# A gated attention kernel: x in contiguous chunks, three rows a head in one transfer, and a new order at the end

## The chip, the cores and the metric

The kernel runs on one core of one Trainium2 chip. The metric is device time in microseconds (us), the median of several executions. One execution was also recorded by the hardware profiler, and every line of a profile below comes from such a recorded execution. The engines are TensorE (PE, with its weight loads PEld), VectorE (DVE), ScalarE (ACT), GpSimd (POOL) and SyncE (SP), which here only issues transfers.

## The reference

With S = 2048 tokens, D = 512 features and 32 heads of 16:

```python
g = sigmoid((x * gate_w).sum(-1, keepdims=True))
qkv = x @ wqkv                                   # 512 -> 3 * 512
p = softmax(q @ k.T * 16 ** -0.5)                # per head, 2048 x 2048
a = concat_heads(p @ v) @ wo
r = x @ w_r
idx = argsort(-r)[:2]                            # two tokens of all
y = (silu(x[idx] @ w_gate) * (x[idx] @ w_up)) @ w_down * sigmoid(r[idx])
b = x; b[idx] += y
out = g * a + (1 - g) * b
```

Everything is float32, in and out.

## The kernel before, in words

Projections, the output product and the low-order corrections are made of pairs of float32r tiles: a value is split into a high part (`hi`, a copy by ACT into float32r) and a low part (`lo`, the value minus `hi`, by VectorE or GpSimd). A product is then three matmuls: hi x hi, hi x lo, lo x hi. `split` (L68) is that helper; `pool_split` (L76) does both parts on GpSimd.

The order of instructions is written out by hand; nothing is reordered later, so each engine's queue runs in the order in which the Python code issues.

**Start.** 14 matmuls on a zero tile `warm` (L228) keep TensorE busy while the first loads run. `load_w(0)` (L112) loads the weights of k, then x's first block (`load_x(0)`, L135), then the weights of q. x is kept transposed, features on partitions, in four blocks of 512 tokens (`nb`), each of four chunks of 128 features (`c`); a chunk is 256 KB, and in DRAM its 128 rows of 2 KB lay 8 KB apart. All of these are issued by SP. `split_x` (L140) makes the high and low parts of a block, the low part of chunk 3 on GpSimd, the others on VectorE. `proj0` (L221) is one projection of 128 columns for one block: twelve matmuls, first the eight that need only x's high parts (two a chunk), then the four with its low parts; it goes into one of three rotating PSUM banks (`st`). In this order come k0, q0, k1, k2, k3, q1, q2 (the digit is the block). After each, ACT writes the high part and VectorE the low part of the result (`ev`, `evx`), which is the only reader of the PSUM bank. `first_rows` (L209) copies the rows of the first two heads from there straight into the attention tiles `Kx[0]` and `Qx[0]`, some of them from GpSimd's queue; `store_ev` (L190) stores everything to DRAM scratch (`qk_scr`), from which later heads are loaded. The weights of V (`wvs`) are split after k1's projection, the low parts in turn on VectorE and GpSimd; the high parts lie in `Kx[1]`.

**Attention tiles.** A head takes 48 partitions in `Kx` (k high, k low, k high) and in `Qx` (q high, q high, q low), so that one matmul over 48 rows gives all three products; two more rows carry the negated row maxima. Two heads form a pair (partitions 0 and 64), and a pair is done in two units of 1024 queries. In DRAM scratch the high and the low parts were two separate planes, so that `load_k` (L257) and `load_q` (L266) needed two transfers a head: one of 32 rows, one of 16.

**Lead phase** (steps -21 to -1, 27 to 90 us). TensorE takes in turn score matmuls for the first maxima (`m_lead`, L609), the last projection of the first group (q3) and the products for V (`v_part`, L291, three a step). Beside it GpSimd multiplies the x rows (`xn`, from `load_rows`, L313) with the router and gate weights (`products`, L322), and ACT sums them (`sums`); TensorE reads the sums in `r_row` (L339, matmul L341) at the last step.

**Main loop** (512 steps of 128 keys). A hand-written pattern (`ORDER`) mixes score matmuls (L669, exponentials on ACT at L670), score matmuls for the maxima 21 steps ahead (L589, reduced on VectorE at L593), the products with V (L679) and filler work: the projections of the other three groups, the routed tokens' layers, the output product. Maxima go through `m_rows` (L652), eight small transfers on SP for each unit. `evict` (L201) stores a projected group part; `split_at` (L498) prepares a group of attention outputs for the output product, on GpSimd.

**End.** `tail` (L780) handles the last unit: the last three products of tiles 10, 11 and 9 for what is already there (`late_wo`), the normalisation of the last heads' outputs, their split, and their product with `wz` (L820) for tiles 12 to 15, three matmuls a tile. `finish` (L557) is one VectorE operation that adds a tile from PSUM; `acc_add` (L471) does the same by ACT and GpSimd. `store` (L561) writes a 256 KB tile of the output.

## Time and profile before

| | |
|---|---|
| median of 3 runs | 1420.77 us (1420.66 to 1420.93) |
| profiled execution | 1419.9 us, span of the trace 1417.9 us |
| mean granted TensorE clock | 0.999 |
| PE busy | 1410.2 us (99%) |
| DVE busy | 1288.8 us (91%) |
| ACT busy | 1170.9 us (83%) |
| POOL busy | 320.4 us (23%) |
| moved by DMA | 92.87 MB, 65 GB/s over the span |

The profiled execution's time lies 2.0 us above its span: the span runs from the first to the last event that the trace holds. Lines of the timeline and of the chain begin with the start and the length in us; `x4` is a merged run of four instructions; what stands in brackets is the engine's idle time before it and what ended that. Rows of a wait list give the total, the number and the longest. Rows of the table by stage give the length of the stage, then busy time (and instructions) of PE, PEld, DVE, ACT and POOL, the granted clock, the mean busy share of the 16 DMA engines, and GB/s.

### The profile page before, as it was taken

Reading aid. Unit: us, or ns where it says so; the run is one execution under the profiler, and the core shown is the slowest. Engines: PE = TensorE matmul, PEld = TensorE weight load, DVE = VectorE, ACT = ScalarE, POOL = GpSimd, SP = SyncE. Lnnn points to the kernel's source line nnn. Section 1 sums busy time; section 2 is a strip of 40 time slices with the busy share of each in tenths; the row PEclk is TensorE's granted clock in tenths of the full one; section 3 lists DMA queues with packets and bytes.
Section 4 is the critical chain, followed back from the end, with each engine's and each line's share of the span. In section 5 each row is a group of like instructions: output and inputs, shape, how many; then the busy total and the mean of one; then the engine's idle time right before and its main releaser. Section 6 shows DMA issues by size and latency. Waiting matters only on the chain.

```text
span 1417.9 us, 24172 instructions
## 1 busy us (share of the span) xinstructions
PE 1410.2 (99%) x9113; PEld 630.7 (44%) x9113; DVE 1288.8 (91%) x1532; ACT 1170.9 (83%) x2276; POOL 320.4 (23%) x337
## 2 busy tenths in 40 slices
PE   9999999999999999999999999999999999999998
PEld 6654444444444444444444444434444444444433
DVE  6889999999999999999999999999999999999943
ACT  5568888888888888888888888888888888888986
POOL 4851101102000001200000100043722322234411
PEclk9999999999999999999999999999999999999999
DMA  8601121212223221312222332424322131012012
GB/s 242 235 27 51 30 42 31 66 34 51 46 64 97 62 54 31 68 30 65 58 83 54 87 82 78 105 58 120 83 46 54 34 69 28 26 31 58 10 35 93
DMA packets 51592, 92.87 MB, mean 65 GB/s; under 512 B 14208, under 2 KB 21376, under 8 KB 49844
## 3 DMA queue, kind: packets, MB, share of 16 engines
q1 hardware_dynamic: 51188, 91.02, 24.4%
q8 instruction: 72, 1.18, 0.4%
q0 software_dynamic: 288, 0.30, 0.1%
q14 instruction: 44, 0.36, 0.1%
HBM read 63.77 MB, written 28.57 MB: 65 GB/s over the span
## 4 chain that ended last, share of the span: by engine, by line
PE 98%; DVE 0%; DMA 0%; ACT 0%; SPq 0%; issue 0%; POOL 0%; DVEq 0%; ACTq 0%
PE av L679 36%; PE st L669 24%; PE mxa L589 12%; PE mxb L589 10%; PE fl L154 6%; PE fl L508 4%; PE st L298 3%; PE st L154 2%; PE mxa L624 1%; PE fl L399 1%; DMA xs<-xT 0%; PE fl L437 0%; DVE acc L559 0%; DVE Mr L593 0%; PE mxa L508 0%; PE mxb L624 0%
## 5 line engine op out<-in xcount | busy, mean ns | idle before, releaser
L670 ACT ACTIVATE P<-st 128x512 f32<-128x512 f32 x2028 | 1065.6, 599 | 191.4 <-PE st L669 108.0
L593 DVE TENSOR_REDUCE Mr<-mxa 128x2 f32<-128x1024 f32 x655 | 795.7, 1215 | 2.6 <-PE mxa L589 2.5
L679 PE MATMUL av<-P,V 128*32 128x512 f32 x4096 | 545.6, 605 | 0.0
L669 PE MATMUL st<-Qx,Kx 50*128 50x512 f32 x2028 | 536.5, 444 | 0.8 <-ACT P L670 0.6
L593 DVE TENSOR_REDUCE Mr<-mxb 128x1 f32<-128x512 f32 x654 | 450.9, 689 | 61.0 <-PE st L669 17.1
L669 PEld LDWEIGHTS st<-Qx,Kx 50*128 50x128 f32 x2028 | 279.0, 184 | 239.6 <-ACT P L670 223.8
L589 PE MATMUL mxb<-Kx,Qx 48*128 48x512 f32 x654 | 325.1, 497 | 0.0
L589 PE MATMUL mxa<-Kx,Qx 48*128 48x512 f32 x1310 | 294.7, 417 | 0.0
L589 PEld LDWEIGHTS mxb<-Kx,Qx 48*128 48x128 f32 x654 | 119.5, 183 | 273.7 <-DVE Mr L593 273.7
L589 PEld LDWEIGHTS mxa<-Kx,Qx 48*128 48x128 f32 x1310 | 124.8, 183 | 43.6 <-DVE Mr L593 2.6
L679 PEld LDWEIGHTS av<-P,V 128*32 128x32 f32 x4096 | 81.2, 108 | 139.3 <-issue 133.2
L205 POOL TENSOR_SCALAR ev<-pe 128x512 fp32r<-128x512 f32 x24 | 35.7, 1490 | 411.6 <-ACT pe L203 411.6
L475 POOL TENSOR_TENSOR acc<-acc,w 128x512 f32<-128x512 f32 x36 | 46.1, 1280 | 202.1 <-ACT w L474 202.0
L77 POOL TENSOR_SCALAR hl<-m 128x16 fp32r<-128x16 f32 x31 | 7.8, 252 | 294.1 <-DVE m L640 294.1
L154 PE MATMUL fl<-xh,wh 128*128 128x512 f32 x96 | 42.9, 447 | 0.0
L154 PE MATMUL fl<-xh,wl 128*128 128x512 f32 x96 | 40.4, 421 | 0.0
L508 PE MATMUL fl<-woh,ahl 128*128 128x512 f32 x96 | 35.2, 447 | 0.0
L559 DVE SCALAR_TENSOR_TENSOR acc<-fl,gg,acc 128x512 f32<-128x512 f32 x11 | 8.2, 747 | 27.9 <-PE fl L508 27.9
L629 DVE TENSOR_REDUCE Mr<-mxa 128x2 f32<-128x1024 f32 x21 | 25.7, 1222 | 8.4 <-PE mxa L624 8.4
L154 PE MATMUL fl<-xl,wh 128*128 128x512 f32 x96 | 32.6, 421 | 0.0
L300 ACT ACTIVATE V<-st 128x512 f32<-128x512 f32 x16 | 9.6, 600 | 27.8 <-PE st L298 27.8
L206 POOL TENSOR_TENSOR ev<-pe,ev 128x512 fp32r<-128x512 f32 x24 | 30.8, 1284 | 2.0
(192 smaller groups left out, 780.0 us busy)
## 6 DMA issues: line engine op xcount, KB each, us to landing
q_scr<-ev SPq DMA_DIRECT2D x15, 512.0 KB
Kx<-k_scr SPq DMA_DIRECT2D x30, 256.0 KB
Qx<-q_scr SPq DMA_DIRECT2D x54, 128.0 KB
k_scr<-ev SPq DMA_DIRECT2D x13, 512.0 KB
Qx<-q_scr SPq DMA_DIRECT2D x70, 64.0 KB
xs<-xT SPq DMA_DIRECT2D x16, 256.0 KB
xn<-x SPq DMA_DIRECT2D x4, 1024.0 KB
Qx<-hr SPq DMA_DIRECT2D x256, 2.0 KB
```

The lines of the kernel that those rows point to most:

```text
L154: nc.tensor.matmul(ps, a[:, i, c, :], b[nb][:, c, :], start=n == 0, stop=n == 11)
L205: nc.gpsimd.tensor_scalar(ev[:, 0], t, 1.0, None, op0=OP.mult)
L206: nc.gpsimd.tensor_sub(ev[:, 1], t, ev[:, 0].bitcast(F32))
L298: nc.tensor.matmul(ps, a[nb][:, c, sl], b[:, c, :], start=c == 0 and n == 0, stop=c == 3 and n == 2)
L475: nc.gpsimd.tensor_add(a, a, w)
L508: nc.tensor.matmul(ps, a[:, sl], b[:a.shape[0], c, :], start=first and n == 0, stop=last and n == 2)
L589: nc.tensor.matmul(dst, Qx[u % 3][64 * j:64 * j + 48, t * 128:t * 128 + 128], k_of(u, t // 4)[64 * j:64 * j + 48, c * 512:c * 512 + 512], ...
L593: nc.vector.tensor_reduce(Mr[:, g0:g0 + (2 if r == 1 else 1)], MX[r - 1], axis=AX.X, op=OP.max, negate=True)
L629: nc.vector.tensor_reduce(*r, axis=AX.X, op=OP.max, negate=True)
L669: nc.tensor.matmul(ps, k, q, start=True, stop=True)
L670: nc.scalar.activation(P[s][:, 2 * j + c, :], ps, AF.Exp)
L679: nc.tensor.matmul(AV[0][32 * ct:32 * ct + 32, :], V[:, kt, h * VW:h * VW + 32], P[s][:, ct, :], start=kt == 0, stop=kt == KT - 1)
```

## The change

1. x lies in DRAM so that each chunk of 128 features by 512 tokens is one contiguous 256 KB; of the first block, chunks 0 and 2 are issued by ACT, the others by SP as before.
2. All low parts of x are made by VectorE. V's weights are split later, two chunks after k2's projection and two after k3's, the low parts all on GpSimd.
3. Ten warming matmuls instead of fourteen.
4. The scratch of q and k holds a head's rows as they stand in the attention tiles, three for each feature (k: high, low, high; q: high, high, low). `store_ev` therefore writes three rows where it wrote two, in two transfers; `load_k` and `load_q` fetch a head with one transfer of 48 rows. The first pair's q keeps the order that `first_rows` gives its k, with two transfers.
5. At the end: tile 11 is added by `finish` and not by `acc_add`; the matmuls of tiles 12 and 13 with the high parts come first; the last tile is added and stored in two halves, one from ACT's queue, one from SP's.
6. The first `split_at` is issued three steps later.

```diff
-    qk_scr = {n: dram.tile([2, D, S], F32R, name=f"{n}_scr") for n in "qk"}
+    qk_scr = {n: dram.tile([D, 3, S], F32R, name=f"{n}_scr") for n in "qk"}
...
-            nc.sync.dma_start(xst[nb][:, c], ap(xT, c * 128 * S + nb * 512, [[S, 128], [1, 512]]))
+            eng = nc.scalar if nb == 0 and c % 2 == 0 else nc.sync
+            eng.dma_start(xst[nb][:, c], ap(xT, (nb * 4 + c) * 128 * 512, [[512, 128], [1, 512]]))
...
-            split(xh[nb][:, c], xl[nb][:, c], xst[nb][:, c], lo_engine=nc.gpsimd if c == 3 else None)
+            split(xh[nb][:, c], xl[nb][:, c], xst[nb][:, c])
...
-        nc.sync.dma_start(
-            ap(qk_scr[which], g * 128 * S + nb * 512, [[S, 128], [D * S, 2], [1, 512]]).bitcast(F32), ev.bitcast(F32))
+        e = ev.bitcast(F32)
+        for i, src in ((0, e), (2, e[:, 0, :])) if which == "k" else ((0, e[:, 0:1, :].to_broadcast([128, 2, 512])), (2, e[:, 1, :])):
+            d = ap(qk_scr[which], (g * 384 + i) * S + nb * 512, [[3 * S, 128], [S, 2 - i // 2], [1, 512]])
+            nc.sync.dma_start(d.bitcast(F32), src)
...
-    for _ in range(14):
+    for _ in range(10):
...
-    for c in range(4):
-        split(wv[1][:, c], wv[2][:, c], wvs[:, c], lo_engine=nc.gpsimd if c % 2 else None)
...
-            o = (g * 128 + r + 16 * j) * S
+            o = (g * 128 + r + 16 * j) * 3 * S
-            nc.sync.dma_start(t[64 * j:64 * j + 32, :], ap(qk_scr["k"], o, [[S, 16], [D * S, 2], [1, S]]).bitcast(F32))
-            nc.sync.dma_start(t[64 * j + 32:64 * j + 48, :], ap(qk_scr["k"], o, [[S, 16], [1, S]]).bitcast(F32))
+            nc.sync.dma_start(t[64 * j:64 * j + 48, :], ap(qk_scr["k"], o, [[S, 48], [1, S]]).bitcast(F32))
...
-                nc.sync.dma_start(t[64 * j:64 * j + 32], ap(qk_scr["q"], o, [[S, 16], [0, 2], [1, n]]).bitcast(F32))
-                nc.sync.dma_start(t[64 * j + 32:64 * j + 48], ap(qk_scr["q"], D * S + o, [[S, 16], [1, n]]).bitcast(F32))
+                if pair:
+                    nc.sync.dma_start(t[64 * j:64 * j + 48], ap(qk_scr["q"], o, [[S, 48], [1, n]]).bitcast(F32))
+                else:
+                    nc.sync.dma_start(t[64 * j:64 * j + 32], ap(qk_scr["q"], o, [[3 * S, 16], [S, 2], [1, n]]).bitcast(F32))
+                    nc.sync.dma_start(t[64 * j + 32:64 * j + 48], ap(qk_scr["q"], o + 2 * S, [[3 * S, 16], [1, n]]).bitcast(F32))
...
-        acc_add(11, pw[1], gg)
+        finish(11, pw[1])
...
-        for t in range(4):
-            for n, (a, b) in enumerate(((0, 0), (1, 0), (0, 1))):
-                nc.tensor.matmul(banks[t], hl[a][:, t * 128:t * 128 + 128], wz[0][:, b, :], start=n == 0, stop=n == 2)
-            finish(12 + t, banks[t])
-            store(12 + t)
+        for t, n in ((0, 0), (0, 1), (1, 0), (1, 1), (0, 2), (1, 2), (2, 0), (2, 1), (2, 2), (3, 0), (3, 1), (3, 2)):
+            a, b = ((0, 0), (0, 1), (1, 0))[n]
+            nc.tensor.matmul(banks[t], hl[a][:, t * 128:t * 128 + 128], wz[0][:, b, :], start=n == 0, stop=n == 2)
+            if n == 2 and t < 3:
+                finish(12 + t, banks[t])
+                store(12 + t)
+        a = acc[3][:, 3, :]
+        for i, eng in enumerate((nc.scalar, nc.sync)):
+            c = slice(256 * i, 256 * i + 256)
+            nc.vector.scalar_tensor_tensor(a[:, c], banks[3][:, c], gg[:, 15:16], a[:, c], op0=OP.mult, op1=OP.add)
+            eng.dma_start(out[15 * 128:, c], a[:, c])
...
-        at_step(now[0] + 10, split_at, 0, (0, 1))
+        at_step(now[0] + 13, split_at, 0, (0, 1))
...
     for w, nb in (("k", 2), ("k", 3), ("q", 1), ("q", 2)):
         proj0(w, nb)
+        if w == "k":
+            for c in (2 * nb - 4, 2 * nb - 3):
+                split(wv[1][:, c], wv[2][:, c], wvs[:, c], lo_engine=nc.gpsimd)
...
-        "xT": np.ascontiguousarray(x.T), "x": x, "wqkv": wqkv,
+        "xT": np.ascontiguousarray(x.T.reshape(4, 128, 4, 512).transpose(2, 0, 1, 3)), "x": x, "wqkv": wqkv,
```

More of the change, by code (lines that the diff above doesn't have):

```diff
@@ L271, in load_q @@
             for j in range(2):
-                o = (pair * 32 + 16 * j) * S + q0
+                o = (pair * 32 + 16 * j) * 3 * S + q0
                 t = Qx[u % 3][:, i * n:i * n + n].bitcast(F32)
-                nc.sync.dma_start(t[64 * j:64 * j + 32], ap(qk_scr["q"], o, [[S, 16], [0, 2], [1, n]]).bitcast(F32))
-                nc.sync.dma_start(t[64 * j + 32:64 * j + 48], ap(qk_scr["q"], D * S + o, [[S, 16], [1, n]]).bitcast(F32))
+                if pair:
[3 more added lines that the diff above has]
+                    nc.sync.dma_start(t[64 * j + 32:64 * j + 48], ap(qk_scr["q"], o + 2 * S, [[3 * S, 16], [1, n]]).bitcast(F32))
     def k_of(u, c):
```

## The prediction

> **What bounds the kernel now.** I read the page first, then the waits of TensorE, the table by stage, and the chain that ended last in order of time.
>
> ```profile
> span 1417.9 us, 24172 instructions
> PE 1410.2 (99%) x9113; PEld 630.7 (44%) x9113; DVE 1288.8 (91%) x1532; ACT 1170.9 (83%) x2276; POOL 320.4 (23%) x337
> PE 98%; DVE 0%; DMA 0%; ACT 0%; SPq 0%; issue 0%; POOL 0%; DVEq 0%; ACTq 0%
> ```
> ```profile
> PE st L229 <- DVE warm L226: 1.2, 1, 1.2
> PE st L669 <- ACT P L670: 0.6, 2, 0.4
> PE st L154 <- ACT xh L70: 0.6, 1, 0.6
> PE st L820 <- DVE onl L71: 0.3, 1, 0.3
> ```
> ```profile
> 200.00:600.00 400.00, 400.00 (x2647) 174.65 (x2639) 380.35 (x443) 337.49 (x651) 50.88 (x54) 1.00 0.22 53
> ```
> ```profile
> 2.59 5.46 DMA xs<-xT
> 8.07 0.64 ACT xh L70
> 8.75 18.58 PE st L154 x78
> 27.33 0.43 PE mxa L624 x2
> ```
>
> TensorE is on the chain for 98% of it and idle for 1417.9 - 1410.2 = 7.7 us in all; from 200 to 600 us it has no gap. The whole list of its waits is 2.7 us long, and two of the four lie where the change works: the first projection waits for x, the last product waits for VectorE. The chain starts with the first x block's last chunk landing at 8.05 and is TensorE from 8.75 on. So a gain can come from the first 27 us and the last 10 us alone, and the middle can only be harmed.
>
> **The start, up to 27 us.** Four stalls are to be priced.
>
> ```profile
> 1.18 5.33 PE L229 MATMUL st<-warm 128*128 128x512 bf16 x14 [1.18 <-DVE warm L226]
> 3.46 0.63 ACT L70 ACTIVATE wh<-ws 128x512 fp32r<-128x512 f32 x1 [1.45 <-DMA ws<-wqkv]
> 4.57 1.95 PE L229 MATMUL st<-warm 128*128 128x512 bf16 x6
> 8.78 1.29 POOL L71 TENSOR_TENSOR xl<-xs,xh 128x512 fp32r<-128x512 f32 x1 [3.14 <-ACT xh L70]
> 9.50 1.12 DVE L71 TENSOR_TENSOR wl<-ws,wh 128x512 fp32r<-128x512 f32 x1 [1.40 <-ACT wh L70]
> 10.10 2.68 ACT L70 ACTIVATE xh<-xs 128x512 fp32r<-128x512 f32 x4 [0.63 <-DMA xs<-xT]
> 10.46 0.40 PE L154 MATMUL st<-xh,wh 128*128 128x512 f32 x1
> 10.76 2.06 DVE L71 TENSOR_TENSOR xl<-xs,xh 128x512 fp32r<-128x512 f32 x3
> 13.30 0.39 PE L154 MATMUL st<-xh,wh 128*128 128x512 f32 x1
> 16.02 0.39 PE L154 MATMUL st<-xh,wh 128*128 128x512 f32 x1
> 18.74 0.68 DVE L74 SCALAR_TENSOR_TENSOR evx<-st,evx 128x512 fp32r<-128x512 f32 x1
> 20.52 2.19 ACT L70 ACTIVATE Kx<-wvs 128x512 fp32r<-128x512 f32 x4 [1.95 <-DMA wvs<-wqkv]
> 21.46 0.39 PE L154 MATMUL st<-xh,wh 128*128 128x512 f32 x1
> 24.30 0.50 PE L154 MATMUL st<-xh,wh 128*128 128x512 f32 x1
> ```
>
> The rows at 10.46, 13.30, 16.02, 21.46 and 24.30 are first products of projections (q0, k1, k2, q1, q2). Undisturbed, one takes 16.02 - 13.30 = 2.72 us, so a product takes 0.227.
>
> *Warm-up.* The first eight of fourteen start 4.57 - 1.18 = 3.39 us before the ninth, 0.424 each; the last six take 1.95, so the rate doubles inside them. Ten end at about 1.18 + 10 x 0.424 = 5.42. The chain does not run through them but through 8.05, so the four that go are worth nothing unless x comes sooner. Then they stop being a lid.
>
> *Last low part of the first block.* Call A the landing of that chunk (8.05 now). Its high part is there at A + 0.70; six products are left (two with it, four with low parts), so k0 can end at A + 0.70 + 6 x 0.227 = A + 2.06 = 10.11. It ends at 10.46, since GpSimd's low part takes 1.29 from 8.78. VectorE does the same form in 2.06 / 3 = 0.69, done at about 9.44, before the last product is due. Gain 0.35. The wk low part, still on VectorE, does not stand in its way.
>
> *q0.* 13.30 - 10.46 = 2.84, 0.12 too long: wq's low part takes 1.12 beside GpSimd's. Without GpSimd I price it at 0.69, behind the low part above, done at A + 2.1; its first use is at A + 2.29. Gain 0.12, with 0.2 of cover. Without that cover it costs up to 0.12 again.
>
> *q2.* 24.30 - 21.46 = 2.84, again 0.12 too long, behind evictions that VectorE could only begin after its share of V's low parts (ACT's high parts were held by the V weights' landing at 20.5). With these on GpSimd and later, gain 0.12.
>
> *A itself.* The windows show the transfer rate:
>
> ```profile
> 2.00:3.00 1.00, 1.00 (x4) 0.44 (x3) 0.00 (x0) 0.01 (x1) 0.95 (x2) 1.00 0.93 268
> 7.00:8.00 1.00, 1.00 (x4) 0.36 (x3) 1.00 (x2) 0.37 (x1) 0.00 (x0) 1.00 0.99 252
> 10.00:11.00 1.00, 1.00 (x4) 0.59 (x4) 0.86 (x2) 0.86 (x2) 0.07 (x1) 1.00 1.03 395
> ```
>
> The last number is GB/s. wk's part and the four chunks are 5 x 262 KB = 1.31 MB. At 395 GB/s from 2.0 us they would be in by 5.3; ACT then sets the pace: its five high parts of 0.63 from 3.46, where wk's part is in, end at 6.6, which is what A = 5.95 would give. That is the early end. The late end: the engines are already 0.93 to 0.99 busy, and ACT now issues two transfers ahead of its first work while wk's part shares the engines with chunk 0; I allow 0.3, A = 8.35. No row tells whether contiguous 256 KB reads go faster than 2 KB rows 8 KB apart: the 8 KB spacing itself ran at 395 later, which speaks for the late end; two queues keep two transfers open on each engine in the slow stretch, which speaks for the early one. I take the middle, A = 7.2, worth 0.85.
>
> The Trainium skill speaks against this part: "DMA: Bandwidth & Descriptors", section "Issuing engines are not separate DMA queues", says that transfers from different issuing engines end on the same 16 engines and that a second queue saves only the issuing time. By that, A stays at 8.05 and the sum loses 0.85; the share of 0.93 to 0.99 agrees.
>
> *VectorE as the new lid.* It now does four low parts a block, not three. From x1's first low part (10.76) to k1's eviction stand 12 + 3 operations of 0.67 to 0.69: 10.05 to 10.35, so k1's PSUM bank is free at 20.8 to 21.1 (now 19.42, from the row at 18.74). q1 takes that bank (three banks, in turn) and would start at 21.46 - 0.35 - 0.85 - 0.12 = 20.14. If x1 lands 0.85 sooner with the rest, the bank is free at 19.95 to 20.25: no stall or 0.1. If x1 still lands at 10.1, q1 waits to 20.8 or 21.1, and the start is worth 0.36 to 0.66 + 0.12 = 0.5 to 0.8 whatever A does.
>
> Sum of the start: 0.35 + 0.12 + 0.12 + 0.85 = 1.4.
>
> **First rows, stores, lead phase.** The rows of k1 for the lead's first reductions go out after that eviction, partly on GpSimd's queue:
>
> ```profile
> Kx<-evx POOLq DMA_DIRECT2D x2, 32.0 KB, 3.9
> ```
> ```profile
> 40.01 1.28 POOL L325 TENSOR_TENSOR p<-xn,wr 128x512 f32<-128x512 f32 x1 [12.83 <-DMA xn<-x]
> 88.45 0.19 ACT L329 ACTIVATION_READ_ACCUMULATOR p<-p 128x1 f32 x1
> 89.47 0.27 PE L341 MATMUL fl<-cst,gz 128*16 128x128 f32 x1
> ```
>
> Bank free at 20.1, two issues of about 0.6 (a row below has one on SP), landing 3.9 after the second began: 24.6 to 25.2, and TensorE wants them at 27.3 - 1.4 = 25.9. Hidden by 0.7. V's low parts, four of 1.29, begin once ACT has V's high parts, near 21, and with four row issues of 0.6 queued between them on GpSimd end near 28.6. V's products follow the lead's first reductions and twelve products of q3, so at about 25.9 + 0.9 + 2.7 = 29.5, and the last chunk's one lead step later. Hidden; if the V weights land later still, what is late next is that first V product.
>
> A store now is two issues and 768 KB instead of 512 KB: for k0 and q0, 0.52 MB more go ahead of the x rows on SP's queue, 2.1 us at 252 GB/s plus two issues of 0.6: 3.3. GpSimd's products can bear most of that: 32 x 1.28 and two weight parts of 1.29 from 40.01 would end at 83.6, the last sum is out at 88.64, so about 5 us of that chain is idling or the last sums, which I count at 0.8; TensorE, 0.8 behind it, comes 1.4 sooner. Cover 5.0 - 0.8 + 0.8 - 1.4 = 3.6 against 3.3, which itself starts sooner: priced at nothing, with a rival below.
>
> **Middle.** Loads fall from four issues to two for each K pair and each Q part, and stores rise from one to two.
>
> ```profile
> 330.73 5.28 SPq L660 DMA_DIRECT2D Qx<-hr  x8
> 343.79 0.60 SPq L263 DMA_DIRECT2D Kx<-k_scr  x1
> ```
>
> The tightest thing on SP is the row of maxima (L660): its eight issues end at 336.0, and the unit that reads them starts where the next K load is issued, at 343.8. One more store issue ahead costs 0.6 of these 7 us; the waiting store itself, with these rows behind it, waits no longer than now, since GpSimd's eviction is unchanged. K and Q parts land two units ahead. The move of one split by three steps (10 to 13) leaves it eight steps ahead of its use on a GpSimd that is 23% busy. All at zero; without that cover a unit would stall by what its rows are late.
>
> **End.**
>
> ```profile
> 1407.94 0.69 ACT L474 ACTIVATE w<-mxa,gg 128x512 f32<-128x512 f32 x1 [0.22 <-PE mxa L508]
> 1408.60 0.42 DVE L810 TENSOR_TENSOR o<-o,mxb 128x256 f32<-128x256 f32 x1 [0.99 <-PE mxb L807]
> 1413.17 0.75 DVE L559 SCALAR_TENSOR_TENSOR acc<-mxb,gg,acc 128x512 f32<-128x512 f32 x1
> ```
> ```profile
> 1414.00:1414.50 0.50, 0.00 (x0) 0.00 (x0) 0.00 (x0) 0.00 (x0) 0.00 (x0) 1.00 1.03 381
> 1416.00:1416.50 0.50, 0.00 (x0) 0.00 (x0) 0.00 (x0) 0.00 (x0) 0.00 (x0) 0.50 0.18 66
> ```
>
> Tile 11 moves to VectorE: 0.75 from 1407.94 delays the first multiply from 1408.60 to about 1408.72, 0.12 lost. High parts first fills TensorE's wait for VectorE (0.3 in the list), but tile 12 is now complete with the fifth product, not the third: 0.45 later less 0.3, and the same four VectorE operations follow it, the last of 0.75 from 1413.17 now cut in two. So they end 0.1 to 0.4 later. Behind them the transfer engines are full to 1416.1: the last five stores are 1.31 MB, 3.4 us at 381 GB/s. Halving the last store changes no byte of that, and the later VectorE hides behind the queue of stores. I take 0, between 0.3 lost (a later start, 1 KB rows) and 0.3 gained (a shorter last piece).
>
> **Sum.** 1.4 + 0 + 0 + 0. The profiled run took 1419.9 us for its span of 1417.9, the runs' median is 1420.77; 1.4 off gives a profiled run of 1418.5 and a median of 1419.4.
>
> **Rivals.**
> 1. *The loads reach their later rate at once* (A = 5.95 or less). For it: 395 GB/s two microseconds later, from the same tensor. Against: the engines are already near full at 252. Gain 0.35 + 2.1 + 0.24 = 2.7, with the end 0.3 better 3.0: 1418.1 to 1417.8. Chance 0.17.
> 2. *The chunks bring nothing*: A stays where the full engines put it, and VectorE's 15 operations hold q1. Gain 0.5 to 0.8: 1420.1. For it: the busy share; against: 252 is not the rate at which the same rows went later. Chance 0.14. This is the case of the Trainium skill's section named above.
> 3. *Slower: the heavier stores hold the x rows*, GpSimd's products finish after TensorE's read. It decides once the first x rows land over 5.0 us later, when the stall eats the 1.4. If the extra 0.52 MB goes at a third of the 252 GB/s (6.2 + 1.2 = 7.4), TensorE stands 3.8 at L341: net 2.4 slower, 1423.2. For it: the twelve microseconds of GpSimd's wait for x rows. Against: the rows of k1 to q1 and the x rows themselves are most of that queue, and the earlier evictions let it start sooner. Chance 0.09.
>
> The forecast (gain 0.8 to 2.3, 1418.5 to 1420.0) keeps 0.60. 0.2% is 2.84 us, about what a measurement of this kernel can tell from no change. Over that on the fast side lie half of rival 1 (0.09) and 0.05 of the forecast's own error: 0.14. On the slow side lie the worst third of rival 3 (0.03) and 0.04 of stalls that no row shows: 0.07. Same: 0.79. The range reaches from rival 1's better end (1417.6) to the near side of rival 3, a stall of 1.6 (1421.0).
>
> **What would show it.** Right: the first block's last chunk lands near 7.2, k0 ends near 9.3, q1 starts near 20.1, the lead's first reduction near 25.9; TensorE's total idle shrinks mainly at "ACT xh". Wrong, fast: A near 6. Wrong, none: q1 waits for VectorE's eviction. Wrong, slow: a TensorE wait at L341, or at L624 for Kx rows, or at L669 in the middle. At the end, transfers full until about 1.8 us before the last.

## The result, and the profile after

The changed kernel took 1417.29 us (median of 10 runs, 1416.82 to 1418.26), the kernel before on the same chip 1420.39 (10 runs, 1419.80 to 1421.91): a ratio of 0.9978, 95% interval 0.9968 to 0.9987. The gain is 3.1 us; 1.4 were forecast, and the time lies 0.3 below the predicted range. The two profiled executions, 1419.9 and 1417.53, differ by only 2.4: the kernel before's lies 0.5 below its median, the changed kernel's 0.24 above its own.

The page of the changed kernel (the q lines are the transfer queues: packets, MB, share of 16 engines) and TensorE's whole wait list:

```profile
span 1415.8 us, 24079 instructions
PE 1408.3 (99%) x9109; PEld 629.4 (44%) x9109; DVE 1288.4 (91%) x1536; ACT 1170.5 (83%) x2275; POOL 315.4 (22%) x334
q1 hardware_dynamic: 53940, 98.75, 24.7%
q10 hardware_dynamic: 432, 0.66, 0.1%
```
```profile
PE st L232 <- DVE warm L229: 1.2, 1, 1.2
PE st L672 <- ACT P L673: 0.6, 2, 0.4
PE st L155 <- ACT xh L70: 0.4, 1, 0.4
```

The last product's wait for VectorE (0.3 before) is gone. The start, in the chain, the table by stage, and the timeline:

```profile
0.74 4.07 DMA ws<-wqkv
4.83 0.63 ACT wh L70
6.04 19.76 PE st L155 x84
```
```profile
2.00:3.00 1.00, 1.00 (x4) 0.44 (x3) 0.00 (x0) 0.94 (x1) 0.95 (x2) 1.00 0.33 123
3.00:4.00 1.00, 1.00 (x4) 0.32 (x3) 0.00 (x0) 0.00 (x0) 1.00 (x1) 1.00 0.99 383
4.00:5.00 1.00, 1.00 (x4) 0.30 (x2) 0.00 (x0) 0.17 (x1) 0.94 (x2) 1.00 1.05 406
5.00:6.00 1.00, 0.63 (x2) 0.00 (x0) 0.51 (x1) 0.98 (x2) 0.63 (x2) 1.00 1.06 408
```
```profile
5.37 2.39 ACT L70 ACTIVATE xh<-xs 128x512 fp32r<-128x512 f32 x4
9.29 0.40 PE L155 MATMUL st<-xh,wh 128*128 128x512 f32 x1
12.03 0.39 PE L155 MATMUL st<-xh,wh 128*128 128x512 f32 x1
20.20 0.39 PE L155 MATMUL st<-xh,wh 128*128 128x512 f32 x1
22.91 0.39 PE L155 MATMUL st<-xh,wh 128*128 128x512 f32 x1
25.73 0.50 PE L627 MATMUL mxa<-Kx,Qx 48*128 48x512 f32 x2
87.95 0.27 PE L344 MATMUL fl<-cst,gz 128*16 128x128 f32 x1
```

The transfers run at 383 to 408 GB/s from 3 to 6 us and at 332 to 379 until 11, where they ran at 234 to 272 (with one microsecond at 346) until 9. By the semaphore updates in the two traces (a transfer has landed with its sixteenth) x's last chunk landed at 6.92 instead of 8.05. The chain no longer begins with it but with the weights' first part (`wk`), which now goes at the same time as chunk 0: it landed at 4.81 instead of 3.44, and ScalarE takes it at 4.83 instead of 3.46. The first products stand 1.17 (q0, at 9.29), 1.27 (k1), 1.26 (q1), 1.39 (q2) and 1.53 us (lead) earlier than before; `r_row` keeps 1.52. So the start gave 1.53 in this pair of executions.

The middle gained too, although TensorE had and has no gap in it:

```profile
200.00:600.00 400.00, 400.00 (x2646) 174.52 (x2647) 380.66 (x444) 338.04 (x651) 51.74 (x54) 1.00 0.23 62
```

As a ruler I take the "stretch", from VectorE's first `m<-Mr` (the last reduction of a unit's maxima) to the 32nd. Before it ran from the first to the second of these rows:

```profile
74.95 0.22 DVE L640 TENSOR_REDUCE m<-Mr 128x16 f32<-128x64 f32 x1
1357.73 0.22 DVE L640 TENSOR_REDUCE m<-Mr 128x16 f32<-128x64 f32 x1
```

that is 1282.78 us; after it takes 0.34 less, gathered over many units. From the last products with V to the end of the last addition it takes 11.80 us before, 11.77 after. The last rows:

```profile
1400.26 3.04 PE L682 MATMUL av<-P,V 128*32 128x512 f32 x24
1411.17 0.86 DVE L830 SCALAR_TENSOR_TENSOR acc<-mxb,gg,acc 128x256 f32<-128x256 f32 x2
1414.00:1414.50 0.50, 0.00 (x0) 0.00 (x0) 0.00 (x0) 0.00 (x0) 0.00 (x0) 0.50 0.77 258
1414.50:1415.00 0.50, 0.00 (x0) 0.00 (x0) 0.00 (x0) 0.00 (x0) 0.00 (x0) 0.50 0.00 0
```

From the last addition to the end of the span, however, it takes 3.73 us instead of 4.01. There SyncE goes through its waits for the last stores, one line of the wait list before and one after:

```profile
SPq L1048 <- DMA out<-acc: 2.2, 1, 2.2
```
```profile
SPq L1060 <- DMA out<-acc: 1.9, 4, 0.8
```

Before, one wait took all of it and the other semaphores were gone through behind it; after, most of them were gone through while the stores still ran. So the 2.4 us between the two profiled executions are 1.53 at the start, 0.34 in the stretch, 0.28 behind the last addition and some 0.2 outside the span.

### The profile page after: what moved, and what is told of

It is laid out like the page before. It is cut to its first block, busy times and chain, and to the rows that moved or that the text cites. A ratio compares the mean times of both kernels' runs of the same rounds, so it can differ in the third digit from the quotient of the medians.

```text
span 1415.8 us, 24079 instructions
## 1 busy us (share of the span) xinstructions
PE 1408.3 (99%) x9109; PEld 629.4 (44%) x9109; DVE 1288.4 (91%) x1536; ACT 1170.5 (83%) x2275; POOL 315.4 (22%) x334
## 4 chain that ended last, share of the span: by engine, by line
PE 99%; DVE 0%; DMA 0%; ACT 0%; issue 0%; POOL 0%; DVEq 0%
PE av L682 36%; PE st L672 24%; PE mxa L592 12%; PE mxb L592 10%; PE fl L155 6%; PE fl L511 4%; PE st L301 3%; PE st L155 2%; PE mxa L627 1%; PE fl L402 1%; DMA ws<-wqkv 0%; PE fl L440 0%; DVE acc L562 0%; DVE Mr L596 0%; PE mxa L511 0%; PE mxb L627 0%
```

## The experiments

"Gain" is the median of the kernel before less the kernel's own, with both on the same chip in the same series (the kernel before's median was 1420.0 to 1420.8 from series to series). "Lead" is the first product of the lead's first reduction, "stretch" the change of the ruler above, both from the profiled execution; "span" is the median span of all executions, and "rest" the median time outside it. The 95% interval of a ratio reaches about 1.3 us to either side. A smaller difference between two of these kernels is not settled by it; such a difference rests on the ranges of the executions and on the profiles.

| kernel | median (range) | gain | ratio, 95% | span | rest | lead | stretch |
|---|---|---|---|---|---|---|---|
| before | 1420.39 (1419.8-1421.9) | 0 | | 1418.0-1418.9 | 1.97 | 27.26 | 0 |
| after | 1417.29 (1416.8-1418.3) | 3.10 | 0.9968-0.9987 | 1415.45 | 1.78 | 25.73 | -0.34 |
| e1 one queue | 1417.30 (1416.8-1418.0) | 2.83 | 0.9972-0.9990 | 1415.5 | 1.79 | 25.89 | -0.68 |
| e2 spaced rows | 1418.06 (1416.8-1418.9) | 2.07 | 0.9974-0.9992 | 1416.2 | 1.78 | 25.99 | -0.37 |
| e15 old load | 1418.70 (1417.7-1419.7) | 1.84 | 0.9975-0.9993 | 1416.8 | 1.78 | 28.61 | -1.16 |
| e8 halves | 1419.74 (1418.6-1420.2) | 0.64 | 0.9984-1.0002 | 1417.9 | 1.82 | 28.36 | -0.66 |
| e3 chunks alone | 1419.86 (1419.1-1420.3) | 0.27 | 0.9987-1.0005 | 1417.9 | 2.00 | 27.10 | +0.18 |
| e14 + two queues | 1419.68 (1418.4-1421.1) | 0.86 | 0.9984-1.0002 | 1417.7 | 1.97 | 25.75 | +0.03 |
| e13 chunks, V late | 1419.27 (1418.8-1419.9) | 1.27 | 0.9981-0.9999 | 1417.0 | 2.25 | 26.59 | -0.12 |
| e16 queues, V late | 1419.13 (1418.8-1419.6) | 1.55 | 0.9979-0.9997 | 1416.9 | 2.23 | 26.10 | +0.19 |
| e17 queues, x low | 1418.60 (1418.1-1419.4) | 2.08 | 0.9975-0.9993 | 1416.8 | 1.79 | 25.71 | +0.34 |
| e5 V early | 1417.15 (1416.8-1418.2) | 3.23 | 0.9970-0.9988 | 1415.4 | 1.78 | 25.54 | -0.68 |
| e9 x low on GpSimd | 1417.22 (1417.0-1417.3) | 2.78 | 0.9971-0.9989 | 1415.2 | 1.99 | 25.65 | -0.78 |
| e4 old scratch | 1418.01 (1417.6-1418.4) | 2.12 | 0.9974-0.9992 | 1416.2 | 1.86 | 25.44 | +0.20 |
| e4b scratch alone | 1420.13 (1418.8-1423.2) | 0.25 | 0.9992-1.0010 | 1418.3 | 1.92 | 27.26 | -0.72 |
| e10 two loads | 1417.77 (1417.5-1418.1) | 2.23 | 0.9975-0.9993 | 1416.0 | 1.81 | 25.44 | -0.12 |
| e11 four loads | 1419.21 (1418.8-1419.6) | 0.79 | 0.9986-1.0004 | 1417.4 | 1.81 | 25.40 | +0.54 |
| e6 old end | 1417.01 (1416.8-1418.1) | 3.37 | 0.9968-0.9987 | 1415.1 | 1.86 | 25.42 | -0.72 |
| e7 14 warm | 1417.54 (1417.1-1418.5) | 3.27 | 0.9966-0.9985 | 1415.75 | 1.81 | 25.65 | -0.31 |
| e12 combined | 1417.79 (1417.1-1418.7) | 2.21 | 0.9976-0.9994 | 1416.0 | 1.79 | 26.35 | -1.03 |

### Loading x

**One queue**, in the changed kernel:

```diff
-            eng = nc.scalar if nb == 0 and c % 2 == 0 else nc.sync
+            eng = nc.sync
```

> The changed kernel with all chunks of x issued by SP; x still contiguous. In the changed kernel the transfers ran at 383 to 408 GB/s from 3 us on, the k weights landed at 4.8 and the lead's first reduction began at 25.73. Theory 1 (contiguous chunks set the rate): the rate stays at 380 or more from 3 us on; the k weights no longer share the engines with chunk 0 and land near 3.5 to 4.1, the lead's first reduction comes at 24.7 to 25.2, the median 0.5 to 1.0 us under the changed kernel's. Theory 2 (two open queues set the rate): 250 to 300 GB/s until 9 us as before, last chunk near 8, lead's first reduction near 26.5, median 0.8 us above the changed kernel's.

Within 0.3 of the changed kernel's gain. The weights landed at 3.40, early as in theory 1, but the rate stayed at 260 to 371 GB/s from 2 to 6 us, ScalarE waits 1.3 us for chunk 1, and the lead comes 0.16 later, not earlier. In the changed kernel contiguous chunks alone suffice.

**Spaced rows, two queues** (`ap(xT, c * 128 * S + nb * 512, [[S, 128], [1, 512]])`, as before).

> The changed kernel with x's rows 8 KB apart again, chunks 0 and 2 still from ACT's queue. Theory 1 (contiguity sets the rate): 250 to 300 GB/s until about 9 us, the last chunk near 8, the lead's first reduction near 26.5. Theory 2 (two queues): as the changed kernel, 380 or more from 3 us on, the lead's first reduction at 25.7.

The profiled lead is 0.26 later than after, yet 1.27 earlier than before, with 332 to 402 GB/s from 4 to 8 us. But the median is worse than that: the gain falls from 3.10 to 2.07, where without the second queue it falls to 2.83.

**Old load**: both edits together, all other steps kept.

> The changed kernel with x loaded as before: rows 8 KB apart, all chunks from SP's queue; all other steps stay. With contiguous chunks from one queue, and with spaced rows from two, most of the start's gain stayed (first reduction at 25.89 and 25.99 against 25.73). If either of the two suffices, this kernel loses both: the fourth chunk's high part is ready as late as before, the first projection ends at 10.1 to 10.5, the first reduction starts at 26.6 to 26.9 and the time is 0.9 to 1.2 above the changed kernel's, 1418.2 to 1418.5 (ratio 0.9985 to 0.999). The rival, the fast rate comes from something else of the change (fewer warm-up products, GpSimd idle at the start): the rate is near 400 GB/s from 3 us on, the first reduction starts before 26.2 and the time is within 0.3 of the changed kernel's.

Without either the slow rate is back, and worse than before. The waits and the table by stage of its profiled execution (the column after POOL is the granted clock):

```profile
PE st L155 <- ACT xh L70: 1.6, 1, 1.6
2.00:8.00 6.00, 4.89 (x13) 1.91 (x11) 2.08 (x3) 2.12 (x5) 3.55 (x4) 1.00 0.88 266
8.00:12.00 4.00, 3.53 (x10) 2.57 (x11) 3.41 (x6) 3.62 (x7) 0.00 (x0) 0.70 1.03 381
12.00:16.00 4.00, 4.00 (x17) 3.28 (x16) 4.00 (x7) 3.97 (x8) 0.00 (x0) 0.87 1.07 397
11.43 0.63 PE L155 MATMUL st<-xh,wh 128*128 128x512 f32 x1
11.86 0.63 PE L155 MATMUL st<-xh,wl 128*128 128x512 f32 x1
```

After a wait of 1.6 us at the slow rate the granted clock fell to 0.70, products stand 0.43 apart instead of 0.23, and the lead is 1.35 later than before. With fourteen warm-up products the kernel before had waited 0.59 at a clock of 1.00. The median is 1.4 above the changed kernel's: the loading steps are worth 1.26 (3.10 - 1.84) there. By the medians most of that goes with the contiguous chunks: on top of this kernel the second queue alone gains 0.23 (e2), contiguous chunks alone 0.99 (e1). This kernel's other executions were mostly faster than the profiled 1419.54. The Trainium skill, "TensorE: Matmul & The Clock Gate", section "Part 1: The HAM clock gate (the "warmup" mystery)", has the clock halve after an idle window of some 3.4 us; here a wait of 1.6 us came before the lower clock, so the page's length for it does not fit this trace. A wait of 1.2 us in e2, also behind ten warm-up products, left the clock at 1.00:

```profile
PE st L155 <- ACT xh L70: 1.2, 1, 1.2
```

**Halves**: wk's part and chunks 0 and 1 as two halves of 64 partitions, one on each queue.

> The changed kernel with the k weights and chunks 0 and 1 of the first block each sent in two halves of 64 partitions, one from SP and one from ACT, so that both queues carry the same order; chunks 2 and 3 from SP. Theory 1 (two queues keep the engines full, and the k weights were late only since chunk 0 shared the engines with them): k weights land near 3.6 instead of 4.81, k0 ends at 8.2 to 8.5 instead of 9.29, the lead's first reduction at 24.7 to 25.0, median 0.7 to 1.0 under the changed kernel's. Theory 2 (what counts is when the first transfers start and ACT's own chain, now with three issues and the table load ahead of it): k0 ends at 9.0 to 9.4, median equal.

Neither theory came: the start is slower. The rate stays at 248 to 273 GB/s until 8 us, TensorE waits 1.8 us for `xh` in three parts (1.20, 0.36, 0.25), the granted clock is 0.57 from 8 to 12, and the lead starts at 28.36. These smaller pieces on both queues did not bring the fast rate.

### Which step lets the start's gain through

**Chunks alone**, in the kernel before:

```diff
-            nc.sync.dma_start(xst[nb][:, c], ap(xT, c * 128 * S + nb * 512, [[S, 128], [1, 512]]))
+            nc.sync.dma_start(xst[nb][:, c], ap(xT, (nb * 4 + c) * 128 * 512, [[512, 128], [1, 512]]))
```

> The kernel before with contiguous chunks of x and nothing else. Theory 1: the rate is 380 or more from 3 us on, the last chunk of the first block lands near 6, k0 ends near 8.5 (GpSimd's low part still 1.3 us), and the lead's first reduction comes at 25.3 to 25.8 where it was 27.26: this one line is most of the gain at the start. Theory 2: nothing moves, 27.26.

k0 ends 0.95 earlier (at 9.51, not near 8.5), and q2 gives it back:

```profile
20.37 2.20 ACT L70 ACTIVATE Kx<-wvs 128x512 fp32r<-128x512 f32 x4 [2.46 <-DMA wvs<-wqkv]
22.47 1.55 ACT L73 ACTIVATE evx<-st 128x512 fp32r<-128x512 f32 x3
24.15 0.50 PE L154 MATMUL st<-xh,wh 128*128 128x512 f32 x1 [0.77 <-DVE evx L74]
```

The V weights' split stands ahead of three evictions on ScalarE and waits until 20.37 for its operand; TensorE's bank is late.

**Two queues added** (`(nc.scalar if nb == 0 and c % 2 == 0 else nc.sync).dma_start(...)`), **V late added** to the chunks (the split moved behind k2 and k3, on GpSimd), **both**, and **two queues with x's low parts on VectorE**:

```diff
-    for c in range(4):                                   # after k1   (e13, e16)
-        split(wv[1][:, c], wv[2][:, c], wvs[:, c], lo_engine=nc.gpsimd if c % 2 else None)
+        if w == "k":                                     # after k2, k3
+            for c in (2 * nb - 4, 2 * nb - 3): split(..., lo_engine=nc.gpsimd)
-            split(xh[nb][:, c], ..., lo_engine=nc.gpsimd if c == 3 else None)   # e17
+            split(xh[nb][:, c], ...)
```

> The kernel before with x's first chunks contiguous and from two queues, nothing else changed. Theory A (position of the V weights' split): q1 to q2 still takes over 3.3 us, and the first reduction starts at 26.7 or later, the time is the kernel before's within 0.3. Theory B (landing): the transfers run at some 400 GB/s from 3 us on, the V weights land at about 18.8 as in the changed kernel with the early split, q1 to q2 takes 2.7 to 2.85, the first reduction starts at 25.8 to 26.1 (the first projection 0.95 to 1.2 earlier), and the time is 1418.9 to 1419.2, about 1.2 below the kernel before. x's last low part on GpSimd should cost nothing in either (it cost nothing in the changed kernel).

> The kernel before with the contiguous chunks (one queue) and the late split of the V weights on GpSimd; x's last low part stays on GpSimd, scratch, warm-up and end stay old. The chunks alone gained 0.95 us at the end of the first projection and lost it between q1 and q2 (3.65 us), where ScalarE took the V weights' four high parts in one stretch after they had landed at 20.4. Theory A, it is the position of that split: moved into two portions behind k2 and k3 it lets q1's eviction pass, q1 to q2 takes 2.7 to 2.85, the first reduction starts at 26.2 to 26.4 and the time is 1.0 us below the chunks alone, some 1418.9 (ratio to the kernel before 0.999). Theory B, it is the late landing: with the weights landing at 20 or later ScalarE still comes late to some eviction, the first reduction starts at 26.7 or later and the time is within 0.3 of the kernel before.

> The kernel before with contiguous chunks from two queues and the late split of the V weights on GpSimd; x's last low part stays on GpSimd, scratch, warm-up and end stay old. Without the late split this kernel's profiled execution had the whole start's gain (first reduction at 25.75, span 1416.4), but its 11 executions scatter from 1418.36 to 1421.06 around 1419.68, where the changed kernel's stay within 1.4 us. Theory A, the scatter comes from the V weights' split while it sits ahead of the evictions of k2 and k3 (a late landing holds them): here all executions lie within 1.2 us and the median is 1418.0 to 1418.5 (ratio to the kernel before 0.998 to 0.9986). Theory B, it comes from x's last low part on GpSimd, the late reader of the first chunks: the scatter stays over 2 us and the median at 1419.3 to 1419.9.

> The kernel before with contiguous chunks from two queues and all of x's low parts on VectorE; the V weights are split early, half on GpSimd, as before; scratch, warm-up and end stay old. Theory A (the V weights' split ahead of the evictions makes the scatter): the scatter stays over 2 us, the median at 1419.3 to 1419.9. Theory B (x's low part on GpSimd makes it): all executions within 1.4 us, the median at 1418.0 to 1418.5, as the changed kernel with the V weights split early (1417.15) plus some 0.7 for the old scratch and 0.2 outside the span.

With two queues the V weights land at 18.8, and the profiled execution has the whole gain (lead 25.75, span 1416.4); but the eleven spans run from 1416.4 to 1419.1, and the median, 1419.68, misses theory B's 1418.9 to 1419.2. With the split late the lead comes without the stall (e13: k0 in 3.29 from 6.78, q1 to q2 2.72), though e13's lead, 26.59, and time miss theory A by 0.2 and 0.4; the spans lie within 1.1 us (one queue) and 0.8 (two). With x's low parts on VectorE instead they lie within 1.3. So each of the two theories is half right: in these eleven executions a kernel, the wide scatter with two queues needs GpSimd's low part of x and the early split together, and taking either away is worth 0.7 (the split) to 1.2 us (the low part) in the median. e16 missed the expected median by 0.6, of which 0.26 lies outside the span. What happens in the late executions no profile shows.

**V early** (the changed kernel, the split back after k1) and **x low on GpSimd** (`lo_engine=nc.gpsimd if c == 3 else None` again):

> The changed kernel with V's weights split right after k1's projection again, low parts in turn on VectorE and GpSimd; all else as changed. The prediction's step gives this move 0.12 us. Theory 1 (the wait is tied to the V weights' landing, and grows as the projections come sooner; contiguous chunks alone lost 0.93 there): the projection from q1 to q2 takes 3.4 to 3.7 us instead of 2.71, the lead's first reduction at 26.4 to 26.7, the median 0.7 to 1.0 above the changed kernel's. Theory 2 (0.12): lead's first reduction at 25.9.

> The changed kernel with one step undone: the low part of x's last chunk goes back to GpSimd. My prediction gave this step 0.35 us in the first projection, plus what GpSimd's late low parts cost later. If that holds: the first projection ends near 9.65 instead of 9.29, the first reduction starts 0.35 to 0.8 later (26.1 to 26.5), and the time is 1417.6 to 1418.1. The rival: with the chunks early, GpSimd's part is covered by the other products, the first projection ends within 0.1 of 9.29 and the time is that of the changed kernel (1417.3). In the kernel before with contiguous chunks alone the start's gain was given back between q1 and q2 (3.65 us instead of 2.84): if GpSimd's low parts are what did that, q1 to q2 takes over 3.2 here too; if the late landing of the V weights did it, it stays at 2.7.

Neither step, undone alone, costs the changed kernel anything outside the scatter of the series: the lead at 25.54 and 25.65, the first projection ended at 9.14 in the second. The 0.35 that I gave GpSimd's low part is not there once the chunks come early: in e9 it runs from 7.25 to 8.71 beside other products, and no product waits for it.

### The scratch

**Old scratch** in the changed kernel, **new scratch alone** in the kernel before, and, on the new layout, a head's 48 rows by **two** (32 + 16) and by **four** transfers (16 + 16 + 8 + 8):

```diff
-            nc.sync.dma_start(t[64 * j:64 * j + 48, :], ap(qk_scr["k"], o, [[S, 48], [1, S]])...)
+            for a, n_ in ((0, 32), (32, 16)):        # four: ((0, 16), (16, 16), (32, 8), (40, 8))
+                nc.sync.dma_start(t[64 * j + a:64 * j + a + n_, :], ap(qk_scr["k"], o + a * S, [[S, n_], [1, S]])...)
```

> The changed kernel with the scratch of q and k in two planes and the stores and loads that go with it, as before. Theory A (the scratch is hidden): start as in the changed kernel (25.73), the last products with V of the main loop 1374.5 us after the lead's first reduction as there, time equal within 0.3 us. Theory B (the 0.3 us that the changed kernel gained between the lead and the end comes from fewer issues on SP): that stretch is 1374.86 as before, time 0.3 us above the changed kernel's.

> The kernel before with only the scratch of q and k changed (three rows a feature, two stores, one load a head). From the first unit's maxima to the last unit's, the three kernels with the new scratch took 0.34 to 0.68 us less than the kernel before, the two with the old one 0.18 to 0.20 more. Theory A (the scratch shortens the main loop): that stretch is 0.3 to 0.7 us shorter here too, the start unchanged (lead's first reduction 27.2 to 27.3), the median 0.3 to 0.7 lower. Theory B (another part does it, or single executions scatter so much): the stretch within 0.2 of before.

> The changed kernel, with its three-row scratch kept, but every head's 48 rows loaded again by two transfers (32 rows and 16 rows). The stretch from VectorE's first row maximum to its 32nd is 1282.78 us in the kernel before; kernels with the old scratch took +0.18 and +0.20 against that, kernels with the new one -0.34 to -0.72. Theory A, the stretch is shorter because fewer load transfers are issued and moved: the stretch comes back to 0 to +0.2, the time is 0.5 to 0.7 above the changed kernel's, some 1418.0 (ratio to the kernel before 0.9983). Theory B, it is the layout (three rows of a head side by side in memory, and the stores that go with it): the stretch stays at -0.3 to -0.7, the time within 0.3 of the changed kernel's.

> The changed kernel, with every head's 48 rows loaded by four transfers (16, 16, 8 and 8 rows), the layout kept: a second dose of the same. Theory A (number of transfers): the stretch from the first row maximum to the 32nd grows by about twice the dose of the kernel with two transfers, to +0.5 or more above the kernel before, and the time comes to about 1419. Theory B (layout): the stretch stays at -0.3 to -0.7 and the time within 0.3 of the changed kernel's. A third reading, the stretch differs by chance from program to program: no order by the number of transfers.

The loads from scratch of the changed kernel and of the one with four transfers, in the DMA lists (transfers, KB each):

```profile
Kx<-k_scr SPq DMA_DIRECT2D x30, 384.0 KB
Qx<-q_scr SPq DMA_DIRECT2D x52, 192.0 KB
Qx<-q_scr SPq DMA_DIRECT2D x16, 96.0 KB
Qx<-q_scr SPq DMA_DIRECT2D x2, 128.0 KB
Qx<-q_scr SPq DMA_DIRECT2D x2, 64.0 KB
```
```profile
Kx<-k_scr SPq DMA_DIRECT2D x60, 128.0 KB
Qx<-q_scr SPq DMA_DIRECT2D x106, 64.0 KB
Qx<-q_scr SPq DMA_DIRECT2D x136, 32.0 KB
Kx<-k_scr SPq DMA_DIRECT2D x60, 64.0 KB
Qx<-q_scr SPq DMA_DIRECT2D x32, 16.0 KB
Qx<-q_scr SPq DMA_DIRECT2D x2, 128.0 KB
```

These are 102 and 396 transfers; two a head make 200, as before. The stretch orders by that number without overlap: -0.31 to -1.16 in all eleven profiles with 102, -0.12 to +0.34 in all eight with 200, +0.54 with 396. The bytes and the layout are the same in after, e10 and e11, so it is the number of load transfers, or the fewer rows in each that go with it: the gain falls from 3.10 to 2.23 and 0.79. On the chip of e10 and e11 the executions of e9 (102 loads, 1417.0 to 1417.3), of e10 (1417.5 to 1418.1) and of e11 (1418.8 to 1419.6) do not overlap (e12's, with 102 loads but a later start, run from 1417.1 to 1418.7). TensorE shows no wait for it: idle inside the stretch it is 0.80 us before and after, 0.82 in e10 and e11.

The two doses are 0.87 us for 98 transfers and 1.44 for 196, but not all of that lies beside TensorE. From the last addition to the span's end it takes 3.66 to 3.73 us in ten of the eleven profiles with 102 loads (4.03 in e8), 3.99 to 4.06 in all eight with 200, and 4.51 with 396; the old end with 102 loads (e6) has 3.67, the new end with 200 (e4, e10) 4.06. So 0.33 and 0.45 of the two doses are waits behind the last product, and what is left is, as an estimate, some 5 ns a transfer; the single profiles' stretches (-0.34, -0.12, +0.54) give only 2 to 3.

New scratch alone shows the shorter stretch (-0.72), and its profiled execution, 1418.78, is the fastest of its eleven; but its median gains 0.25 in a scatter of 4.4 us: why that does not add up is open.

### The end, the warm-up, and a combination

**Old end**, in the changed kernel:

```diff
-        finish(11, pw[1])
+        acc_add(11, pw[1], gg)
-        for t, n in ((0, 0), (0, 1), (1, 0), (1, 1), (0, 2), ...):   # and the halved last addition
+        for t in range(4):
+            for n, (a, b) in enumerate(((0, 0), (1, 0), (0, 1))): ...
+            finish(12 + t, banks[t]); store(12 + t)
```

> The changed kernel with the end as before (tile 11 by ScalarE and GpSimd, three products a tile in turn, one last store). Theory 1 (the prediction: the end is held by the queue of stores): from the last products with V to the span's end 15.5 to 15.8 us both ways, median within 0.1. Theory 2 (the halved last store shortens the drain): 15.8 here against 15.5, and the time outside the span 2.0 instead of 1.75: median 0.4 to 0.5 above the changed kernel's.

The median is 0.3 better than the changed kernel's, within the scatter: the new end is worth nothing. No run undoes the later `split_at`.

**Fourteen warm-up products** in the changed kernel (`for _ in range(14)` at L231).

> The changed kernel with fourteen warm-up products instead of ten. My prediction gave the four products no worth, since the first part of x was not there when ten had ended. In the kernels with early chunks and fourteen products those ended at 5.96 to 7.08 and the first projection began at 5.65 to 6.73, up to 1.1 us after its operands were ready (some 5.6), while ten end at 5.0 to 5.6. Theory A, fourteen are now the limit of the start: the first projection begins at 6.2 to 6.8 with no wait on ScalarE before it, ends at 9.2 to 9.8, the first reduction starts at 25.7 to 26.3, and the median is 0.3 to 0.7 above the changed kernel's, 1417.6 to 1418.0 (ratio to the kernel before 0.998 to 0.9985). Theory B, worth nothing: the same start as the changed kernel within 0.15 (9.29 and 25.73), and a median within 0.2 of 1417.3.

The start is that of ten (6.18, then 9.22 and 25.65), and the gain is the same: worth nothing, as forecast. Its profiled execution, 1418.53, is the slowest of its ten and shows how a microsecond is lost:

```profile
23.17 2.31 SPq L195 DMA_DIRECT2D q_scr<-ev  x2
27.49 0.60 ACT L73 ACTIVATE ev<-st 128x512 fp32r<-128x512 f32 x1 [3.86 <-DMA k_scr<-ev]
30.00 0.51 PE L627 MATMUL mxa<-Kx,Qx 48*128 48x512 f32 x2 [0.66 <-DVE Mr L632]
```

The heavier stores hold an eviction buffer until 27.5, ScalarE's next eviction and VectorE behind it are 1.7 late, and from the lead to `r_row` it takes 63.26 us, not 62.22.

**Combined**, the edits of e1, e5 and e6 in one kernel: chunks from one queue, x's low parts on VectorE, ten warm-up products, new scratch; V split early, old end.

> The changed kernel reduced to the parts that the runs so far gave a worth: the contiguous chunks (all from SP's queue), x's low parts on VectorE, ten warm-up products and the new scratch; the second queue is gone, the V weights are split early on both engines as before, and the end is the old one. If the parts add up, each of the three removed is worth 0 to -0.3 and the time is 1416.8 to 1417.3, no worse than the changed kernel (ratio to the kernel before 0.9975 to 0.998), with the first reduction's first product at 25.4 to 25.9. If the second queue or the late split covers for something that the other alone does not: the V weights' high parts or q1 come later, the first reduction's first product is at 26.5 or later, and the time is 1418 or more.

The parts do not add up: without the second queue 2.83, with the early split 3.23, without the end 3.37, without all three 2.21. The lead, 26.35, and the time, 1417.79, lie between the two forecasts. At 266 to 342 GB/s until 8 us the V weights land at 19.66; that the second queue and the late split cover for each other would fit, but it is not shown apart. No kernel here beats the changed one by more than the series differ.

## Why the prediction was wrong, by its own steps

- **"The middle can only be harmed", priced at zero: this step failed.** It was read from a TensorE that is busy 400.00 of 400 us. Undoing the scratch takes back 0.98 (e4), loading its heads in two transfers again 0.87 (e10); the number of load transfers orders the length of the stretch, and 0.3 of the worth lies behind the last addition. A TensorE without gaps said nothing of how closely its products follow each other, nor of the waits behind the last one.
- **The start's sum, 1.4: right in the profile (1.53), too small in the median.** In e17 loading and x's low parts on VectorE together gain 2.08, some 0.2 of it outside the span, where the profiled lead moved by 1.55; with V's late split in place of the low parts (e16) it is 1.55. The sum was made from one execution of the kernel before and its lower stalls; the others scatter upward by up to 2.9 us of span, and in e16 and e17 a low-part step narrows that scatter. I gave these steps 0.35 + 0.12 + 0.12; with two queues they are worth 0.7 (V) or 1.2 (x), once, not both. e17's 2.08 and the scratch's 0.9 to 1.0 make up the 3.1.
- **A, the landing at 7.2: near (6.92), and what it should have given was lost elsewhere.** By A + 2.06 the first projection would have ended at 8.98; it ended at 9.29. `wk`'s part came 1.37 later than before, where I had allowed 0.3, and from 4.83 on ScalarE's five high parts follow each other almost without a gap, so that the last begins at 7.14 and ends at 7.76. That 9.29 is so near to the forecast 9.3 is in part luck: the earlier landing and the late weights cancel.
- **The rule that a second queue saves only issuing time** (the Trainium skill, "DMA: Bandwidth & Descriptors", section "Issuing engines are not separate DMA queues"): with contiguous chunks the trace agrees in the median (2.83 with one queue, 3.10 with two). With spaced rows a second queue raised the profiled rate between 4 and 8 us from 199 to 305 GB/s (e15) to 332 to 402 (e2), and x's last chunk landed at 7.33 instead of 8.41, which the page does not lead one to expect; the median gained only 0.23 by it. A did not stay at 8.05.
- **VectorE as the new lid** did not bind: q1 at 20.20, forecast 20.14, with no wait.
- **Warm-up and end at zero: right** (e7, e6). The transfers were full until some 1.4 us before the last event; I had said 1.8.
- **Rival 1** named 1417.8 to 1418.1 and came nearest, but only in its number: the last chunk landed at 6.92, not at 5.95 or less, and the lead moved 1.53, not 2.7. The range's lower end, 1417.6, lies 0.2 beyond that rival's own best sum. **Rival 2** fell (k0 ended 1.17 earlier). **Rival 3**, the heavier stores, showed in e7's profiled execution at another place, 1.0 us, not 3.8.
- **TensorE's idle time** was to shrink mainly at "ACT xh". It fell only from 7.7 to 7.5 us, 0.2 of it there; the rest of the profiled gain stands as shorter busy time, 1410.2 to 1408.3.
- **0.19 us lie outside the span** (1.97 before, 1.78 after); I had assumed it unchanged.

## What to carry to other kernels

One profiled execution is one draw: before a sum of a microsecond is made from it, its time belongs beside the spread of the others, and a step that takes away the spread is worth more than its stall in the profile. Two steps that each remove the same lateness are worth it once, so each is undone alone and both together before either is credited. And a stage with TensorE at 100% can still get shorter, here by some tenths of a microsecond in 1283, when the transfers beside it get fewer. The bytes moved up to a time do not tell which transfer has landed: in the kernel before, 1.31 MB (the size of `wk`'s part and the four chunks) had moved by 6.7 us, and the last of these chunks landed at 8.05.

## What the hardware showed that was not expected

- The main stretch got longer with the number of load transfers beside a fully busy TensorE (102, 200 and 396 loads of the same bytes: -0.34, -0.12 and +0.54 us in after, e10 and e11), with no wait in the records. The cause is open.
- The rate of the first transfers lay anywhere between some 200 and some 400 GB/s for the same bytes. Contiguous chunks from two queues mostly brought the higher values; one queue with contiguous chunks showed 311, 363, 260, 371 in e1 and 301, 342, 266, 338 in e12 between 2 and 6 us.
- Waits of 1.6 and 1.8 us in all before the first projection was through were followed by mean granted clocks of 0.70 and 0.57 for four microseconds (e15, e8); a wait of 1.2 us was not (e2). All three have ten warm-up products.
- The time outside the span goes with the engine of x's last low part: 1.78 to 1.86 in all thirteen kernels with VectorE, 1.92 to 2.25 in all seven with GpSimd. The traces of those seven, and of none of the thirteen, hold one more transfer of 8 KB behind the last event, of the kind that the profile calls "instruction"; before, between 1417.93 and 1421 us:

```profile
q14 instruction: 1, 0.01, 1.0%
```

It fits as the cause of the longer time, but no run takes it away alone.
